# Block-sparse attention and a gated feed-forward on one core: probabilities turned by DMA transposes, a part of the value gathers issued by GpSimd

## The chip, the cores and the metric

One NeuronCore of a Trainium2 chip runs the whole program. The metric is the device time of one execution in microseconds (us). In the profile PE is TensorE, PEld its weight loads, DVE VectorE, ACT ScalarE, POOL GpSimd and SP SyncE. SP computes nothing here: it issues DMAs.

## The reference

```python
mask = np.abs(blk_i - blk_j) <= 1                       # blocks of 32 positions
mask = mask | (blk_i == 0) | (blk_j == 0) | (blk_i == 23) | (blk_j == 23)
for qb in range(24):
    for kb in sampled_blocks[qb]:                       # three random blocks each
        mask[qb * 32:(qb + 1) * 32, kb * 32:(kb + 1) * 32] = True
scores = np.where(mask, scale * (q @ k.T), -1e9)
attn = softmax(scores) @ v                              # 4 batches, 8 heads, 768 x 64
x = attn.transpose(0, 2, 1, 3).reshape(3072, 512)
out = (sigmoid(x @ w_gate) * (x @ w_val)) @ w_out       # 512 -> 1536 -> 512
```

A query block of 32 rows sees its neighbours, the first and the last block and three sampled blocks; the first and the last query block see everything.

## The kernel before, in words

**The attention of one batch.** Blocks 1 to 22 are done in eleven steps of two query blocks, named by their first block: a step of batch 1 that starts with block 4 is `1_4`. Per step, POOL copies the three sampled key blocks of each query block into a buffer KG beside the window and the two end blocks (`kw`, line 745; `kg`, line 729). PE makes the scores (`sc`, lines 790 and 801): 256 keys per query block, two PSUM banks of 128 rows (4 pairs of heads by 32 queries) each. DVE takes the row maxima (`mx`, 815), ACT the exponentials with their sums (`ex`, 826) into one of three buffers P, and DVE or ACT divides by the sums (`sl`, 850 and 848). The probabilities then have to stand with the keys on the partitions. In batches 0 to 2 PE does that with eight 128x128 transposes into PSUM (`tp`, 870), and DVE or ACT copies them to one of three buffers PTS (`te`, 876). In batch 3 one DMA transpose from P to PTS does it, issued by SP (line 858). Last PE multiplies with the values (`pv`, 888), and the result goes into XT or XL, the transposed input of the feed-forward (`xe`, 914).

**The values.** Each batch is written in token order to a DRAM tensor `scr` (615). V1A to V1D hold four windows of 96 rows each (`w`, 692), and V2A to V2D the sampled rows: for each query block three DMAs of 32 rows from `scr`, issued by SP, their addresses read from registers (`vg`, 762).

**The dense blocks.** Blocks 0 and 23 have scores against all 768 keys (`dsc`, 941), maxima, exponentials, a division (953, 959, 968), per block two sets of six PE transposes (`dtp`, 976; eight in batch 0) with a copy each to DPT (`dte`, 985), and a product with all values (`dpv`, 998; 1006 in batch 0). In batches 1 to 3 value tokens stand six to a partition, so that partition p holds tokens 6p to 6p+5 (eight in batch 0); the scores read the keys with that step and write them with the tokens of one slot together.

**Keys and queries** of batches 1 to 3 are loaded one or two batches ahead by POOL (437), put in row order (`rr`, 556, on POOL or DVE), turned on PE (571) and copied to KT and QT (586 to 590).

**The feed-forward** takes the tokens in nine groups of 1, 1, 2, 2, 2, 4, 4, 4 and 4 tiles of 128: twelve pairs of products with `wg` and `wv` (1061), a tanh (1070), a product on DVE (1075), then twelve products with `wo` per tile (1096), a scaling and the store (1110). A group can start only when all its tokens have been through the attention.

**The order** stands in a table, ORDER: one word per operation, its engine, and its buffers by number. Each engine executes its instructions in that order, and tile dependencies make it wait. A number after `+` is a count of filler matmuls ahead of an operation (line 1119), which compute nothing that is used.

Of the kernel before, what the change touches and what calls it, by code (L numbers as in the profile page):

```python
# [18 lines left out]
BLK = 32  # L19
# [44 lines left out]
sc0_12:P01 w0_8:G0 vg0_10:S rz0_8:D dxe0_0:A rz0_10:D sl0_100:D kg0_14:G sl0_101:A mx0_120:D0 vg0_9:S pv0_4:P1+5.7
sl0_80:D wg2:G tp0_10:P22 mx0_121:D xe0_4:A pv0_6:P0 sl0_81:D vg0_8:S ex0_120:A0 xe0_6:D vfl0D:G te0_10:D
pg0_2:P00+4.7 vg0_11:S pu0_2:P1 th0_2:A1 tp0_8:P10 kw0_16:D0 ex0_121:A pg0_0:P00 sc0_14:P03 th0_0:A0 h0_2:D w0_12:S0
kg0_16:G te0_8:A rz0_12:D pu0_0:P0 pg0_3:P10 h0_0:D mx0_140:D2 pu0_3:P0 sl0_120:A wv2:G kw0_18:D1 pv0_8:P1+1.7
kg0_18:G th0_3:A2 regSP0_1:S pg0_1:P10 h0_3:D xe0_8:A pv0_10:P2 mx0_141:D pu0_1:P0 ex0_140:A1 w0_16:G0 vg0_15:S wo0:G
th0_1:A1 xe0_10:A pg0_6:P10+4.7 h0_1:D sl0_121:D wo1:G ex0_141:A sc0_16:P21 vg0_19:S pu0_6:P0 kw0_1:G2 mx0_160:D6
pg1_3:P20 th0_6:A0 vfl0A:G th1_3:A2 pu1_3:P1 h0_6:D ex0_160:A2 pg1_5:P00 vg0_12:S h1_3:D rz0_14:D sc0_18:P30 th1_5:A1  # L70
pu1_5:P2 mx0_180:D4 sl0_141:A tp0_12:P10 pg1_6:P00 h1_5:D pu1_6:P1 te0_12:D regPOOL0_2:G th1_6:A0 pg1_10:P20 vg0_13:S
pu1_10:P0 th1_10:A2 mx0_161:D pg1_2:P20 h1_6:D th1_2:A1 wo2:G h1_10:D ex0_161:A pu1_2:P1+1.4 sl0_140:D vg0_14:S
pg1_0:P00 pu1_0:P2 h1_2:D kw0_2:D0 th1_0:A1 pg0_8:P10 ex0_180:A0 tp0_14:P21 h1_0:D kg0_2:G rz0_16:D sl0_160:D pu0_8:P0
vg0_17:S pg1_4:P20 sl0_161:D th0_8:A2 th1_4:A0 pu1_4:P1 mx0_181:D ldv10:G3 pg1_9:P20 tp0_16:P12 th1_9:A1 h0_8:D
te0_14:A pu1_9:P2 h1_4:D kw0_20:G1 pg0_7:P00 h1_9:D pu0_7:P1 te0_16:D kg0_1:G sc0_2:P13 th0_7:A1 pg0_4:P00 h0_7:D
mx0_20:D5 vg0_18:S pu0_4:P1 th0_4:A0 pg1_11:P20 vfl0B:G pv0_12:P1 mx0_21:D th1_11:A1 ex0_181:A pu1_11:P0 pg1_7:P20
h0_4:D vg0_16:S h1_11:D pu1_7:P1 xe0_12:D pg0_9:P00 th1_7:A0 sc0_1:P20 th0_9:A2 ex0_20:A1 ldk10:G2 rz0_18:D pu0_9:P0
h1_7:D pg1_1:P20 h0_9:D pu1_1:P1 kg0_20:G mx0_10:D1 pg1_8:P00 th1_1:A1 ex0_21:A pu1_8:P2 pv0_14:P1 h1_1:D sl0_180:D
pg0_10:P10 th1_8:A2 ldq10:G1 sl0_181:D th0_10:A0 tp0_18:P00 ex0_10:A2 h1_8:D w0_1:G0 mx0_11:D pu0_10:P1 sc0_20:P14
rz0_2:D sl0_20:D ex0_11:A py1_0:P2 regSP0_2:S mx0_200:D4 w0_2:G0 xe0_14:A h0_10:D te0_18:D ex0_200:A0 mx0_201:D  # L80
sl0_21:D ex0_201:A pv0_16:P2 rz0_1:D vg0_1:S sl0_10:D pg0_11:P10 xe0_16:D pv0_18:P0 th0_11:A0 pu0_11:P0 xe0_18:A
pg0_5:P10 sl0_11:D tp0_2:P11 vg0_3:S h0_11:D ys1_0:A0 vsh1:D0 dsc0_23:P20 th0_5:A1 pu0_5:P0 te0_2:A pg2_0:P20 vg0_20:S
h0_5:D dmx0_230:D6 pu2_0:P1 rrk1:G3 pg2_1:P00 th2_0:A2 pu2_1:P2 h2_0:D dex0_230:A1 dmx0_231:D3 pg2_4:P10 ldv20:G2
trk100:P1 th2_4:A2 trk102:P0 evk100:A regPOOL1_2:G pu2_4:P1 vg0_2:S tp0_1:P22 evk102:A h2_4:D trk101:P1 te0_1:D
pg2_2:P10 th2_1:A2 dex0_231:A0 trk103:P0 scr1:S h2_1:D py0_0:P0 vg0_21:S evk101:D evk103:A rrq1:G3 dsl0_231:D th2_2:A0
vg0_22:S kfl10:G kfl11:G rz0_20:D pu2_2:P2 sl0_200:D ys0_0:A1 trq102:P2 sl0_201:D trq101:P1 h2_2:D evq102:A trq100:P0
kw1_20:D0 pg2_5:P00 evq101:D kw1_1:G1 evq100:A trq103:P2 st0_0:S kg1_1:G pu2_5:P1 evq103:A dsl0_230:D tp0_20:P10
dtp0_230:P00 th2_5:A2 kg1_20:G te0_20:D gv1:S sc1_1:P41 dte0_230:A h2_5:D pg2_3:P20 mx1_10:D3 kw1_2:G1 st1_0:S
pu2_3:P1 th2_3:A2 mx1_11:D regSP1_2:S dtp0_231:P0 ldk20:G1 ex1_10:A1 pv0_2:P2 h2_3:D kg1_2:G dte0_231:D pv0_20:P1
xe0_2:A pg2_7:P20 xe0_20:D pv0_1:P0 regPOOL1_0:G th2_7:A1 pu2_7:P0 w1_1:G0 ex1_11:A vsh2:D3 pg2_9:P20 vg1_22:S  # L90
sc1_2:P02 xe0_1:A h2_7:D pu2_9:P1 kw1_4:G1 mx1_20:D5 pg2_6:P00 vg1_1:S kg1_4:G th2_9:A1 mx1_21:D sc1_20:P31 ex1_20:A2
pu2_6:P2 mx1_200:D2 kw1_6:G0 dpv0_23:P1 vfl1D:S th2_6:A0 h2_9:D kg1_6:G ex1_200:A0 mx1_201:D pg2_10:P00 scr2:S h2_6:D
ex1_21:A pu2_10:P1 rz1_1:D sl1_10:D pg2_8:P20 sl1_11:D th2_10:A2 sc1_4:P03 th2_8:A1 kw1_8:G1 pu2_8:P0 ex1_201:A
mx1_40:D7 w1_2:S0 rrk2:G2 tp1_1:P21 h2_10:D pg2_11:P20 ex1_40:A1 vg1_20:S rz1_20:D dxe0_23:D pu2_11:P1 h2_8:D
th2_11:A0 sc1_6:P10 ldq20:G1 rz1_2:D h2_11:D sl1_20:A pg3_1:P00 vg1_21:S mx1_41:D kg1_8:G pu3_1:P2 th3_1:A2 pg3_0:P10
sl1_21:D sl1_201:D tp1_2:P12 th3_0:A1 mx1_60:D6 pu3_0:P0 vg1_2:S te1_2:A py2_0:P1 kw1_10:D0 te1_1:D vfl1C:G ex1_60:A2
mx1_61:D ex1_41:A vg1_3:S h3_1:D h3_0:D ex1_61:A rz1_4:D kg1_10:G pg3_3:P20 sl1_41:D pv1_1:P0 sl1_200:D ys2_0:A1
sl1_40:D pu3_3:P0 regPOOL1_1:G th3_3:A2 rz1_6:D st2_0:S sl1_61:D sc1_8:P21 xe1_1:A gv2:S sc1_10:P05 kw1_12:G1
mx1_80:D4 pg3_4:P20 w2_2:G0 mx1_81:D tp1_20:P10 th3_4:A0 tp1_4:P01 ex1_80:A0 h3_3:D py2_1:P2 sl1_60:D kg1_12:G
regSP1_0:S mx1_100:D0 ex1_81:A mx1_101:D w1_4:G0 kw1_14:A0 te1_4:D vg1_6:S ex1_100:A1 kg1_14:G rz1_8:D te1_20:D  # L100
pv1_2:P2 ex1_101:A sl1_81:D pu3_4:P0 vg1_4:S w2_1:G0 sl1_80:D pv1_20:P0 xe1_2:A rz1_10:D pg3_2:P10 h3_4:D sl1_100:D
# [134 lines left out]
def kernel(  # L236
# [15 lines left out]
    def pin(x):  # L252
        return tc.keep_in_program_order(x)
# [251 lines left out]
    def pg_of(g):  # L505
        return bk(5, 6) if g < TUNE["two"] else pgb if g < len(GROUPS) - 2 else pgb + bk(4, 3, 2, 1, 0)
# [645 lines left out]
```

## Time and profile before

| | |
|---|---|
| median of 3 runs | 320.91 us (318.99 to 322.62) |
| the profiled execution, its own time | 320.9 us |
| its span, first to last instruction | 319.1 us |
| PE busy | 303.0 us (95% of the span) |
| DVE / ACT / POOL busy | 223.5 / 225.5 / 124.0 us |
| 16 DMA engines, share of the span: POOL's queue / SP's queue | 37.0% / 27.1% |

The span leaves 1.8 us of the execution's own time around it. A busy engine is one with an instruction in flight, and PE's matmuls overlap: a row of 0.61 us for eight transposes is the time from the first's start to the last's end, while the next matmul starts 0.45 us after the first. The chain of waits, which counts from start to start, is therefore the better price for work on PE. The DMA share of a stage is the time that its packets took, divided by 16 engines.

### The profile page before, as it was taken

Reading aid. Unit: us, or ns where it says so; the run is one execution under the profiler, and the core shown is the slowest. Engines: PE = TensorE matmul, PEld = TensorE weight load, DVE = VectorE, ACT = ScalarE, POOL = GpSimd, SP = SyncE. Lnnn points to the kernel's source line nnn. Section 1 sums busy time; section 2 is a strip of 40 time slices with the busy share of each in tenths; the row PEclk is TensorE's granted clock in tenths of the full one; section 3 lists DMA queues with packets and bytes.
Section 4 is the critical chain, followed back from the end, with each engine's and each line's share of the span. In section 5 each row is a group of like instructions: output and inputs, shape, how many; then the busy total and the mean of one; then the engine's idle time right before and its main releaser. Section 6 shows DMA issues by size and latency. Waiting matters only on the chain.

```text
span 319.1 us, 11300 instructions
## 1 busy us (share of the span) xinstructions
PE 303.0 (95%) x4015; PEld 186.3 (58%) x4015; DVE 223.5 (70%) x546; ACT 225.5 (71%) x666; POOL 124.0 (39%) x386
## 2 busy tenths in 40 slices
PE   7999649999999999999999999999999999999996
PEld 3545436867977777886555555556455544554443
DVE  4389435998999999886799788798876676113420
ACT  1469366898898989888799788799985765423411
POOL 7648955705877834815155222221322300000000
PEclk9999787999999999999999999999999999999999
DMA  7998999998699644999543302523455456811012
GB/s 113 206 240 160 230 228 222 215 230 191 135 273 189 202 129 124 160 208 192 165 154 98 106 16 65 178 72 77 116 143 133 98 126 145 159 68 68 0 49 83
DMA packets 50919, 45.99 MB, mean 144 GB/s; under 512 B 18096, under 2 KB 45616, under 8 KB 50768
## 3 DMA queue, kind: packets, MB, share of 16 engines
q0 software_dynamic: 18720, 21.43, 37.0%
q1 hardware_dynamic: 32144, 23.85, 27.1%
q8 instruction: 31, 0.51, 0.7%
q14 instruction: 24, 0.20, 0.2%
HBM read 47.10 MB, written 9.44 MB: 177 GB/s over the span
## 4 chain that ended last, share of the span: by engine, by line
PE 74%; DMA 10%; DVE 7%; ACT 6%; issue 2%; SPq 1%; POOL 0%; ACTq 0%; DVEq 0%; POOLq 0%
PE pall L1061 35%; PE pall L1096 18%; PE pall L888 5%; DMA V2D<-scr 4%; PE pall L801 3%; PE pall L870 3%; ACT P L826 3%; PE pall L571 2%; DMA V2C<-scr 2%; DMA stg<-in_k_dram 2%; DVE NM L815 2%; DMA scr<-XL 2%; PE pall L1119 2%; PE pall L941 2%; DVE P L850 1%
## 5 line engine op out<-in xcount | busy, mean ns | idle before, releaser
L826 ACT ACTIVATE P<-pall,NM 128x256 f16<-128x256 f32 x176 | 81.5, 481 | 5.3 <-DVE NM L815 3.2
L1075 DVE SCALAR_TENSOR_TENSOR HT<-TH,pall 128x512 f16<-128x512 f32 (+2 forms) x108 | 53.0, 504 | 34.4 <-PE pall L1061 24.7
L1070 ACT ACTIVATE TH<-pall 128x512 f32<-128x512 f32 (+2 forms) x108 | 48.5, 460 | 33.9 <-PE pall L1061 29.3
L729 POOL COPY KG<-KT 128x64 f32 x264 | 51.4, 244 | 49.1 <-PE pall L801 27.8
L1096 PE MATMUL pall<-wo,HT 128*128 128x512 f16 (+1 forms) x300 | 65.2, 371 | 0.6 <-DVE HT L1075 0.6
L815 DVE TENSOR_REDUCE NM<-pall 128x2 f32<-128x512 f32 x88 | 58.1, 682 | 5.6 <-PE pall L790 4.7
L1061 PE MATMUL pall<-XT,wv 128*128 128x256 f16 (+2 forms) x336 | 56.5, 291 | 0.9 <-DVE HT L1075 0.7
L1061 PE MATMUL pall<-XT,wg 128*128 128x256 f16 (+2 forms) x336 | 56.2, 291 | 0.4
L1061 PEld LDWEIGHTS <-wg 128*128 128x128 f16 x432 | 38.5, 99 | 26.4 <-issue 3.9
L1061 PEld LDWEIGHTS <-wv 128*128 128x128 f16 x432 | 37.5, 99 | 25.9 <-issue 5.0
L1096 PEld LDWEIGHTS <-HT 128*128 128x128 f16 x300 | 28.5, 98 | 31.3 <-DVE HT L1075 1.1
L826 ACT ACTIVATION_READ_ACCUMULATOR P<-pall,NM 128x1 f32 x176 | 37.3, 212 | 0.0
L850 DVE TENSOR_SCALAR P<-P,ZZ 128x256 f16<-128x256 f16 x140 | 34.8, 305 | 0.7
L1119 PE MATMUL pall<-WZ 128*128 128x512 f16 x83 | 23.2, 424 | 1.2 <-DVE WZ L390 1.2
L1061 PE MATMUL pall<-XL,wg 128*128 128x512 f16 x96 | 23.8, 379 | 0.0
L1061 PE MATMUL pall<-XL,wv 128*128 128x512 f16 x96 | 23.7, 379 | 0.0
L745 POOL COPY KG<-KT 128x384 f32<-128x384 f32 (+1 forms) x27 | 12.5, 475 | 23.5 <-PE pall L790 16.5
L914 ACT CAST XT<-pall 64x256 f16<-64x256 f32 (+1 forms) x48 | 16.3, 340 | 7.4 <-PE pall L888 6.8
L1105 ACT ACTIVATE YS<-pall 128x512 f32<-128x512 f32 (+1 forms) x18 | 10.4, 576 | 15.4 <-PE pall L1096 15.4
L870 PE MATMUL pall<-ident,P 128*128 128x128 f16 x264 | 20.1, 222 | 0.2 <-DVE DPT L985 0.2
L801 PE MATMUL pall<-KG,QT 64*32 64x256 f16 x704 | 18.2, 277 | 1.0 <-ACT DP L959 0.5
L959 ACT ACTIVATE DP<-pall,NM 128x768 f16<-128x768 f32 x16 | 14.4, 904 | 5.7 <-DVE NM L953 5.6
(102 smaller groups left out, 438.3 us busy)
## 6 DMA issues: line engine op xcount, KB each, us to landing
out_dram<-YS SPq DMA_DIRECT2D x23, 256.0 KB, 2.1
stg<-in_q_dram POOLq DMA_DIRECT2D x4, 768.0 KB, 9.4
stg<-in_v_dram POOLq DMA_DIRECT2D x4, 768.0 KB, 8.4
V2C<-scr SPq DMA_DIRECT2D x96, 32.0 KB, 3.0
V2D<-scr SPq DMA_DIRECT2D x78, 32.0 KB, 3.4
stg<-in_k_dram POOLq DMA_DIRECT2D x3, 768.0 KB, 9.2
scr<-stg SPq DMA_DIRECT2D x3, 768.0 KB, 3.4
V1C<-scr POOLq DMA_DIRECT2D x5, 384.0 KB, 4.1
```

The source lines that it names most:

```text
L729: pin(nc.gpsimd.tensor_copy(t[:, :, u, KO[r] + (2 + n) * BLK : KO[r] + (3 + n) * BLK].bitcast(f32), KT[r].bitcast(f32)[:, :, bass.ds(regs[ ...
L801: pin(nc.tensor.matmul(ts[hh][32 * p : 32 * p + 32, u * 256 + c0 : u * 256 + c1], QT[r][kp, p, i * BLK : (i + 1) * BLK], src, start=(merge ...
L815: pin(nc.vector.tensor_reduce(NM[pl.handles[hz][1]][:, 2 * hh : 2 * hh + 2], t, axis=AX.X, op=ALU.max, negate=True))
L826: pin(nc.scalar.activation(pb[:, hh, u, :], t[:, u * 256 : u * 256 + 256], AF.Exp, bias=NM[z][:, 2 * hh + u : 2 * hh + u + 1], scale=1.0, ...
L850: pin(nc.vector.tensor_scalar(pb[:, u, :], in0=pb[:, u, :], scalar1=z[:, 2 * hh + u : 2 * hh + u + 1], scalar2=None, op0=ALU.mult))
L870: pin(nc.tensor.transpose(t[:, m * 128 : m * 128 + 128], pb[:, hh, u, c * 128 : c * 128 + 128], ident))
L914: pin(copy(o)(dst[kp].rearrange("d a (u n) -> d u a n", n=BLK), s[kp, u0:u1]))
L1061: pin(nc.tensor.matmul(t, wt[:, c, f_ * 128 : f_ * 128 + 128], XT[g][:, c, :], start=(c == 0), stop=(c == 3)))
L1070: pin(nc.scalar.activation(TH[o.slots[ht][1]][:, 0:n], banks[pl.handles[hg][1]][:, 0:n], AF.Tanh, bias=0.0, scale=0.5))
L1075: pin(nc.vector.scalar_tensor_tensor(HT[:, f_, hoff : hoff + n], in0=TH[pl.handles[ht][1]][:, 0:n], scalar=1.0, in1=banks[pl.handles[hv][1 ...
L1096: pin(nc.tensor.matmul(t, HT[:, f_, hoff + tt * 128 : hoff + tt * 128 + 128], wo[:, f_, n0:n1], start=(f_ == 0), stop=(f_ == NF - 1)))
L1119: pin(nc.tensor.matmul(banks[o.spare], WZ[:, 0:128], WZ, start=True, stop=True))
```

## The change

Five things change, and the table of the order is new.

1. The probabilities of batches 1 and 2, too, are turned by one DMA transpose per step from SP (`turnby` 'PSSS'); PTS has four buffers in place of three.
2. The dense probabilities of batches 1 to 3 are turned by DMA transposes (`denseby` 'PSSS'): four per batch, 128x768 each, from DP straight into DPT. Batch 0 keeps PE.
3. For batches 1 to 3 the dense scores read 384 keys in a row and write them in a row; the exponential that follows reads PSUM with that step and writes the old order.
4. In batches 1 to 3 a gather of sampled values may be issued by POOL: one indirect DMA of 96 rows, with row numbers from a small table `gidx`, in place of three DMAs from SP. The new order does so for 36 of 66: 15, 12 and 9 in batches 1, 2 and 3.
5. Bank 7 joins the banks of the scores, and bank 4 those of the middle feed-forward groups.

By the new order, 15 of the windows of V1 are issued by SP (4 before) and 9 by POOL (20 before); of the six row-order copies, four are on DVE (all six were on POOL); 80 fillers stand in the table (83 before). `kqby` is 'PPPP', so that keys and queries go the old way.

```diff
- 'npt': 3,
- 'turnby': 'PPPS'}
+ 'npt': 4,
+ 'turnby': 'PSSS',
+ 'gather': 'SEEE',
+ 'denseby': 'PSSS',
+ 'kqby': 'PPPP'}

 ORDER = """
-wz:D cdma:S ldk00:G0 ldk01:G ldq00:G1 ldv00:G2 idx:D memset:G wg0:G mask:D wv0:G trk000:P1+12.7 trk001:P2 evk001:A
...
-    spool = bk(0, 1, 2, 3, 5, 6)
+    spool = bk(0, 1, 2, 3, 5, 6, 7)
...
-        return bk(5, 6) if g < TUNE["two"] else pgb if g < len(GROUPS) - 2 else pgb + bk(4, 3, 2, 1, 0)
+        return bk(5, 6) if g < TUNE["two"] else pgb + bk(4) if g < len(GROUPS) - 2 else pgb + bk(4, 3, 2, 1, 0)
...
+    def f_gix(o):
+        by = flat.rearrange("p (i n) -> p i n", n=3)
+        for n in range(3):
+            ps = slice(BLK * n, BLK * n + BLK)
+            pin(nc.vector.tensor_scalar(gtm[ps], in0=by[ps, :, n], scalar1=float(BLK), scalar2=float(-BLK * n), op0=ALU.mult, op1=ALU.add))
+            pin(nc.vector.tensor_tensor(gidx[ps], gtm[ps], pid[ps], op=ALU.add))
...
                 def f_vg(o, i=i, x=x, ws=ws, key=keys):
+                    if o.eng == "POOL":
+                        pin(nc.gpsimd.indirect_dma_start(V2[x][BLK:128, ws, :], None, scr[b][:, :],
+                                                         bass.IndirectOffsetOnAxis(ap=gidx[0 : 3 * BLK, i : i + 1], axis=0)))
+                        return
                     for n in range(3):
...
-                            ks = ks.rearrange("d (p j) -> d p j", j=TJ)[:, :, TJ // 2 * a : TJ // 2 * (a + 1)]
                             dst = t[32 * p : 32 * p + 32, a, 0:384]
-                            dst = dst.rearrange("q (j p) -> q p j", p=TP)
+                            if b:
+                                ks = ks[:, 384 * a : 384 * a + 384]
+                            else:
+                                ks = ks.rearrange("d (p j) -> d p j", j=TJ)[:, :, TJ // 2 * a : TJ // 2 * (a + 1)]
+                                dst = dst.rearrange("q (j p) -> q p j", p=TP)
...
+                    if b:
+                        dst = DP[o.slots[hDP][1]].rearrange("p (j a n) -> p a j n", j=TJ, a=2)
+                        src = src.rearrange("p a (n j) -> p a j n", j=TJ)
+                    pin(nc.scalar.activation(dst, src, AF.Exp, bias=NM[z][:, 0:1], scale=1.0, accum_out=ZZ[z][:, 0:1]))
...
+                if TUNE["denseby"][b] == "S":
+                    def f_dtd(o, hh=hh, e=e, hDP=hDP, hTS=hTS):
+                        dst = dturn(b, e, (o.slots if hTS in o.slots else pl.handles)[hTS][1])[:, hh]
+                        pin(nc.sync.dma_start(dst.rearrange("p (c n) -> p c n", c=TJ), DP[pl.handles[hDP][1]], transpose=True))
```

Three places of the new order, as the built programs have them (a tile's number after its name tells one buffer from another; ISA is a register instruction).

**SP, the first steps of batch 1, before.** Sampled rows go to V2D and V2C by line 762, the end blocks to V1D and V2D by 648, batch 2's values to `scr` by 615, windows by 692, and line 632 loads the end blocks for POOL's copies.

```order
L632 DMA GV<-scr_127 32x512 x2
L1110 DMA out_dram<-YS_124 128x512
L473 TENSOR_LOAD vidx x2
L762 ISA
L762 DMA V2D<-scr_127 32x512
```

**SP, the same steps, now.** L799 is the gather, L895 the transpose of a step, L724 a window, L680 the end blocks, L664 the ends for POOL's copies.

```order
L664 DMA GV<-scr_129 32x512 x2
L724 DMA V1C<-scr_129 96x2x512 x2
L895 DMA_TRANSPOSE PTS_119<-P_98 128x8x128
L724 DMA V1D<-scr_129 96x512 x2
L680 DMA V1C<-scr_129 32x4x512
L680 DMA V2C<-scr_129 32x4x512
L724 DMA V1A<-scr_130 96x2x512 x2
L895 DMA_TRANSPOSE PTS_117<-P_97 128x8x128
L895 DMA_TRANSPOSE PTS_116<-P_99 128x8x128
L724 DMA V1D<-scr_129 96x4x512
```

The eighteen gathers of these three steps (six query blocks) have left SP, and between the windows stand three transposes, each of which waits for its step's division; what is behind one on SP waits with it.

**SP, the end of batch 1's dense blocks, now.** L1018 is the new dense transpose; before, no instruction of SP belonged to the dense blocks.

```order
L1018 DMA_TRANSPOSE DPT_122<-DP_121 128x6x128
L1018 DMA_TRANSPOSE DPT_122<-DP_120 128x6x128
L895 DMA_TRANSPOSE PTS_116<-P_97 128x8x128
L488 TENSOR_LOAD vidx
L1163 DMA out_dram<-YS_127 128x512
L1018 DMA_TRANSPOSE DPT_122<-DP_121 128x6x128
L1018 DMA_TRANSPOSE DPT_122<-DP_120 128x6x128
```

The two DP buffers are used twice in a row: the second block's exponentials have to wait until the first block's transposes have read them.

**POOL, between the key copies of the fourth and fifth step of batch 1, now.** L761 is the copy of a sampled key block, L795 the indirect gather.

```order
L761 COPY KG_95<-KT_76 128x4x16
L795 DMA V2C<-scr_129,gidx 96x512
L795 DMA V2D<-scr_129,gidx 96x512 x2
L795 DMA V2C<-scr_129,gidx 96x512 x3
L761 ISA
L761 COPY KG_96<-KT_76 128x4x16
```

Six gathers have come in between two sets of key copies, so that the scores of the fifth step wait for them; before, one window copy of keys stood there.

281 lines of the change are left out of this document (152 added, 129 removed).

## The prediction

> **What bounds the kernel now.** I read the page first, then the busy time of each engine by stages of 25 us, then the chain of waits, then the groups of instructions by form, and last the issuing queues of SP and POOL. From the page:
>
> ```profile
> span 319.1 us, 11300 instructions
> PE 303.0 (95%) x4015; PEld 186.3 (58%) x4015; DVE 223.5 (70%) x546; ACT 225.5 (71%) x666; POOL 124.0 (39%) x386
> PE 74%; DMA 10%; DVE 7%; ACT 6%; issue 2%; SPq 1%; POOL 0%; ACTq 0%; DVEq 0%; POOLq 0%
> ```
>
> PE is busy for 95% of the span and holds 74% of the chain. An average can hide stages, so here they are (columns: stage, its length, busy us of PE, PEld, DVE, ACT, POOL with counts, granted clock, share of the DMA engines, GB/s):
>
> ```profile
> 60.00:85.00 25.00, 24.99 (x420) 19.37 (x405) 23.11 (x61) 21.28 (x63) 10.95 (x27) 1.00 0.98 203
> 85.00:110.00 25.00, 24.86 (x458) 18.55 (x457) 24.06 (x67) 23.59 (x86) 19.57 (x60) 1.00 0.93 209
> 110.00:135.00 25.00, 24.50 (x408) 18.84 (x406) 23.08 (x55) 22.63 (x61) 14.61 (x41) 1.00 0.62 135
> 135.00:160.00 25.00, 25.00 (x352) 16.95 (x350) 18.80 (x43) 20.87 (x56) 7.45 (x23) 1.00 0.82 190
> 160.00:185.00 25.00, 24.53 (x295) 13.69 (x293) 20.89 (x49) 21.69 (x65) 10.02 (x37) 1.00 0.40 114
> 260.00:285.00 25.00, 25.00 (x200) 12.79 (x198) 9.62 (x22) 12.68 (x38) 0.68 (x1) 1.00 0.55 126
> ```
>
> From 60 us on PE is never without a matmul for more than half a microsecond in 25, at the full clock. So PE's work sets the end, and what is taken from it comes off the time, as long as nothing else takes its place. Three things are near to doing so between 60 and 135 us, in batch 1: DVE (23 to 24 of 25), ACT (up to 23.6), and the DMA engines (0.98 and 0.93). After 160 us the DMA engines are half idle.
>
> **The turns of P leave PE.** The chain has a set of eight transposes as a piece of its own, and the dense ones, eight or twelve at a time:
>
> ```profile
> 53.38 0.45 PE pall L870 x8
> 84.99 0.45 PE pall L976 x8
> 154.34 0.78 PE pall L976 x12
> ```
>
> Batches 1 and 2 have 22 sets: 22 x 0.45 = 9.9 us off PE. The dense blocks of batches 1 to 3 have 72 transposes; by 0.45/8 they cost 4.0 us, by 0.78/12 4.7, and I take 4.3. The copies that go with them are off DVE and ACT:
>
> ```profile
> L876 DVE COPY PTS<-pall 128x1024 f16<-128x1024 f16 x24 | 16.4, 684 | 1.9 <-PE pall L870 1.7
> L876 ACT COPY PTS<-pall 128x1024 f16<-128x1024 f16 x9 | 9.2, 1017 | 0.7 <-PE pall L870 0.7
> L985 ACT COPY DPT<-pall 128x768 f16<-128x768 f16 x5 | 4.1, 811 | 0.7 <-PE pall L976 0.7
> L985 DVE COPY DPT<-pall 128x768 f16<-128x768 f16 x7 | 3.8, 550 | 0.0
> L603 DVE COPY stg<-stg 128x3072 f16<-128x3072 f16 x3 | 2.9, 955 | 0.0
> ```
>
> DVE loses 17 copies of 0.684 and 7 of 0.550 (15.5 us), and gets four row-order copies of the size of line 603's (3.8 us): 11.7 less. ACT loses 5 x 1.017 and 5 x 0.811: 9.2 less. I cost both at nothing, since PE covers them; what they give is room, so that DVE and ACT can follow a PE that is some 5% quicker through batch 1. Without them PE would be held at their 24 of 25 us there.
>
> **The dense scores read in order.** Rows of PE in time (start, length, matmuls), and the two forms by themselves (minimum, median and maximum in ns):
>
> ```profile
> 92.70 0.41 PE L801 MATMUL pall<-KG,QT 64*32 64x256 f16 x16
> 92.93 0.27 PE L790 MATMUL pall<-mrow,ones 64*32 64x192 bf16 x8
> ...
> 113.64 0.91 PE L941 MATMUL pall<-KT,QT 64*32 64x384 f16 x16
> 114.48 0.61 PE L1061 MATMUL pall<-XT,wv 128*128 128x256 f16 x4
> ```
>
> ```profile
> L941 PE MATMUL pall<-KT,QT x128: 479/493/520, 15.2 to 190.3; 64*32 64x384 f16 x128
> L801 PE MATMUL pall<-KG,QT x704: 266/269/418, 15.8 to 258.1; 64*32 64x256 f16 x176
> ```
>
> Sixteen matmuls over 384 stepped keys hold PE for 114.48 - 113.64 = 0.84 us; sixteen of 256 keys in a row, with the same operand rows, hold it for 0.23. At that rate 384 columns would take 0.35. No row shows 384 in order, and whether the step of the keys, that of the scores or neither makes it slow isn't seen, so six sets save between 0 and 6 x 0.49 = 2.9 us. I take 2.3, near the upper end, as the form in a row is the nearest row. The exponential's stepped read of PSUM has a near row as well: line 586, which gathers such a step out of PSUM on ACT, takes as long as line 985, which doesn't:
>
> ```profile
> L586 ACT COPY KT<-pall 128x768 f16<-128x768 f16 x11 | 8.6, 805 | 7.0 <-PE pall L574 6.7 <-PE pall L571 0.3
> ```
>
> That is 805 against 811 ns, so nothing. Three fillers fewer (0.6 us) lie ahead of 60 us, where PE waits for the DMA of weights and values anyway: nothing. The additional banks only loosen waits.
>
> **The transposes on SP and the DMA engines.** Batch 3 already has eleven:
>
> ```profile
> L858 SPq DMA_TRANSPOSE PTS<-P x11: 1231/1245/1997, 220.1 to 273.4; - x11
> DMA to landing us min/median/max: 2.7/2.8/5.0
> ...
> 240.60:241.70 1.10, 1.10 (x51) 0.62 (x49) 0.13 (x1) 0.54 (x1) 0.08 (x1) 1.00 1.06 238
> ```
>
> One holds SP's queue for 1.25 us, fills all 16 DMA engines for 1.10 x 1.06 = 1.17 us (the third row is a stage with one transpose in it), and has landed 2.8 us after its issue. On SP 22 more make 27.4 us, and 12 dense ones at three quarters of the size between 0.94 and 1.25 each, 11.2 to 15; eleven windows moved from POOL add some 0.4 each. What leaves is 36 gathers:
>
> ```profile
> L762 SPq DMA_DIRECT2D V2C<-scr x96: 315/316/1306, 24.6 to 276.6; - x96
> ...
> 218.72 1.31 SPq L762 DMA_DIRECT2D V2C<-scr  x3
> ```
>
> Three issues with their register work take 1.31 us (the second row, the three of one query block): 36 x 1.31 = 47 us. SP's queue is no fuller than it was. But a transpose waits at its head for the division, and behind it wait the windows and gathers of the next steps, which `pv` on PE needs; I count that into the waits below. The path of one step is longer: eight transposes and a copy (0.45 + 0.68) become 2.8 us or more. In batch 3 no PE wait is put down to a transpose, but there the DMA engines are at half load. How much traffic lengthens a landing is told by the gathers of 32 KB, in 60:85 and in 160:185 (share 0.98 and 0.40):
>
> ```profile
> DMA to landing us min/median/max: 2.1/4.9/6.3
> ```
>
> ```profile
> DMA to landing us min/median/max: 1.6/1.9/3.6
> ```
>
> Three microseconds more. So in batch 1 a transpose should take 3 to 6 us. What is late then is P itself: it has three buffers, and a step's exponentials wait on ACT until the transpose of three steps earlier has been read, with the feed-forward's tanh behind them, for which PE waits. A buffer is used 11/3 = 3.7 times in a batch; each use is 2.8 - 1.13 = 1.7 us longer in quiet, up to 4.9 in traffic. Over two batches that is between 0 (all of it in slack) and, in batch 1 with 4.9 and batch 2 with 1.7, 18 + 6 = 24 us. I take 4, near the lower end: P now waits for its place in PE's order too, and the four PTS buffers and the emptier DVE take up part of it.
>
> **The gathers on POOL.** Nothing in the trace is an indirect DMA. The near rows are POOL's plain DMAs (ns, minimum, median, maximum); the third row is the row-order copy:
>
> ```profile
> L692 POOL DMA_DIRECT2D V1C<-scr x9: 647/677/707, 24.9 to 265.1; - x9
> L692 POOL DMA_DIRECT2D V1D<-scr x9: 541/685/980, 31.0 to 254.5; - x9
> ...
> L556 POOL COPY stg<-stg 128x1536 f32<-128x1536 f32 x6 | 8.8, 1467 | 18.0 <-DVE stg L603 13.0 <-PE pall L571 2.9 <-PE pall L790 2.2
> ```
>
> From 0.54 us below to three plain ones above, 2.0 us; I take 0.9, a little over one plain DMA. Batch 1 is where it matters, with 15 of the 36. In 85:135 POOL is busy for 19.57 + 14.61 = 34.2 of 50 us. Four of its windows (2.7 us) and one row-order copy (1.5) leave; the stage gets some 7 us shorter with PE; so there are 13 us of room, and 15 x 0.9 = 13.5 just fill it. Cost: nothing at 0.9, and 15 x 1.1 = 16 us at 2.0.
>
> **The sum.** Against the span of the profiled execution: 319.1 - 9.9 - 4.3 - 2.3 = 302.6 us if PE stays without gaps, and 306.6 with 4 us of new waits. That execution took 1.8 us more than its span, 320.9, which is the median of the runs (320.91); so 304.4 without and **308.4 us** with the waits.
>
> **Rivals.** *A, all of PE's saving arrives*: 304.4 us. For it: PE has hardly a gap from 60 us on although DVE and ACT are nearly full, and both get emptier. Against it: the longer path above, in the stage with the most traffic.
>
> *C, the DMA engines become the bound in batch 1.* Their shares from 60 to 160 us make 24.5 + 23.3 + 15.5 + 20.5 = 83.8 of 100 us. Some 24 us of transposes (16.4 of batch 1, the rest of batch 2) fall into that time, which itself gets 8 us shorter: 108 in 92. Were all 16 us over to come before PE's operands, the time would be 304.4 + 16 = 320, so about 319 with a little slack, no change. For it: 0.98 and 0.93. Against it: much of the traffic there is loads of batches 2 and 3, which may slip past 160 us. The Trainium skill (DMA: Bandwidth & Descriptors, Queues, rings and completion order) says that each DMA engine takes turns between its queues, a packet at a time; by that a transpose beside a load takes about twice its time, and this case's gathers agree (4.9 against 1.9 us).
>
> *D, POOL becomes the bound in batch 1, slower than before.* If an indirect gather holds POOL for c us, batch 1 lacks 15c - 13 us, the key copies behind the gathers come late, the scores wait for them and PE with them. From c = 0.9 it costs, and from 2.2 it makes the time 304.4 + 20 = 324, slower by over 1%; at 2.5, 329 us. For it: 96 separate rows by index, and DVE nearly full beside it. Against it: POOL's plain DMAs of 96 to 384 rows took 0.54 to 0.98 us, those in the fullest stage too. The Trainium skill (SBUF — State Buffer, A bandwidth-pool intuition that's wrong) has a GpSimd DMA of 620 ns that takes 3100 under a DVE copy; by that the estimate would be 304.4 + 15 x 3.1 - 13 = 338 us. The trace doesn't agree for plain ones: the longest of line 692 on POOL is 0.98 us.
>
> **How the numbers follow.** The forecast (304.4 with 4 us of waits, 305 to 316) gets 0.48, A 0.27, C 0.14, D 0.11. A measurement of this kernel, whose runs lie within 0.6% of their median, can tell about 1% from no change: below 317.7 is faster, above 324.1 slower. The forecast and A are faster, and so is a part of C, 0.03: 0.78 faster, 0.11 the same, 0.11 slower. The range goes from 300 us (the dense scores' full 2.9 us, no waits, and some 3 us from the front of the program, whose order is new and isn't worked out here) to 320, C's upper end; that leaves out D and little else.
>
> **What would show it.** Right: 88 matmuls on the transposing line of P where there were 264, and 32 on the dense one where there were 104; 45 DMA transposes, in batch 1 landing in 3 to 6 us; sixteen dense scores in some 0.4 us; a PE without gaps from 60 us on, and a last feed-forward group that starts some 11 to 16 us earlier. Wrong by C: PE waits for transposes or for the load of batch 3's keys between 75 and 160 us, at a DMA share of 1. Wrong by D: gathers on POOL of 2 us or more, and PE waiting for key copies. The forecast fails if the sum of PE's gaps between 60 and 285 us grows by more than 12 us, or if the matmuls that remain get slower.

## The result, and the profile after

The changed kernel takes 338.11 us (335.07 to 339.15) where the kernel before took 321.56 in the same comparison (318.99 to 322.62): 1.0539 times as long, interval 1.0473 to 1.0605. Slower, where 308.4 was forecast. The profiled execution took 337.09 us. A median below is of all runs of a kernel, while a ratio leaves out runs that fell into a slower state, and is missing where too few are left.

From the page after; the first two rows are span and engines, the third SP's DMA queue (packets, MB, share of 16 engines), the last the shares of the chain:

```profile
span 335.3 us, 10562 instructions
PE 295.3 (88%) x3764; PEld 175.1 (52%) x3764; DVE 215.4 (64%) x526; ACT 217.7 (65%) x659; POOL 149.1 (44%) x409
...
q1 hardware_dynamic: 63584, 32.11, 43.7%
...
PE 56%; DMA 22%; ACT 9%; issue 6%; DVE 4%; SPq 1%; POOL 1%; another core or an unknown queue 0%; POOLq 0%; ACTq 0%; DVEq 0%
```

PE has less to do (295.3 us for 303.0) and stands still for longer: 335.3 - 295.3 = 40.0 us for 16.1. It holds 56% of the chain, no longer 74%; what it lost went to DMA, 22% for 10%. Against the sum's 302.6 us the span is 32.7 longer: 23.9 of idle time, and 8.8 of work (303.0 - 16.5 = 286.5 was the sum's).

The stages of 25 us say where (same columns as before):

```profile
60.00:85.00 25.00, 23.93 (x367) 18.37 (x363) 20.65 (x49) 21.16 (x62) 13.20 (x27) 1.00 1.19 219
85.00:110.00 25.00, 18.68 (x283) 13.83 (x281) 15.64 (x39) 14.45 (x51) 14.09 (x41) 0.86 1.08 202
110.00:135.00 25.00, 20.29 (x347) 13.98 (x345) 19.63 (x53) 18.96 (x63) 15.41 (x46) 1.00 0.93 169
135.00:160.00 25.00, 21.87 (x312) 16.17 (x311) 16.91 (x47) 16.27 (x50) 11.87 (x24) 0.86 1.08 201
160.00:185.00 25.00, 22.73 (x304) 12.85 (x302) 20.28 (x46) 21.00 (x60) 15.69 (x46) 1.00 0.89 190
```

PE idles in every stage, most in batch 1: 6.3 us from 85 to 110. DVE, ACT and POOL are all emptier than before in that stage, so none of them is the bound; the DMA engines are full or nearly so from 85 to 160 us (1.08, 0.93, 1.08 for 0.93, 0.62, 0.82). In two stages the clock is down. By finer stages, the first of these losses:

```profile
97.00:99.00 2.00, 0.00 (x0) 0.00 (x0) 1.27 (x3) 1.02 (x4) 1.70 (x2) 1.00 0.50 128
99.00:101.00 2.00, 0.98 (x8) 0.67 (x7) 1.54 (x4) 0.00 (x0) 1.39 (x3) 1.00 1.10 269
101.00:103.00 2.00, 0.99 (x24) 0.46 (x22) 0.88 (x4) 0.38 (x1) 1.88 (x7) 0.50 1.15 294
103.00:105.00 2.00, 1.84 (x11) 1.27 (x12) 1.49 (x5) 1.72 (x7) 1.61 (x7) 0.50 0.23 66
105.00:107.00 2.00, 2.00 (x14) 1.63 (x13) 2.00 (x8) 1.75 (x6) 0.60 (x1) 0.50 1.36 73
```

After 4 us in which PE was busy for 0.98, the clock is at half for 6 us: a gap is paid for twice. The Trainium skill (TensorE: Matmul & The Clock Gate, Part 1: The HAM clock gate) says that the array's clock is throttled to half by default and that activity releases it; the 0.50 agrees. It puts the idle window at about 3.4 us, and here no single gap was that long: the longest is the 2.84 us before 99.73. Two later falls of the clock, at 135.13 and 145.37 us, came after 3.4 us in which PE was busy for 1.51 and 1.13. So here little work was enough, not only none.

What that gap waited for, in the chain of waits (start, length):

```profile
82.31 14.03 DMA stg<-in_k_dram
...
96.36 0.96 DVE stg L571
97.33 0.60 DVE NM L852
...
98.66 0.70 DVE NM L852
...
99.73 0.60 PE pall L1114 x4
```

A load of the next batch's keys took 14.03 us; before, three such loads took 9.2 in the median (the last figure):

```profile
stg<-in_k_dram POOLq DMA_DIRECT2D x3, 768.0 KB, 9.2
```

Its row-order copy (line 571) now stands in DVE's queue ahead of the maxima of the scores (852), and a product on PE comes behind those. Three more pieces of the same chain are transposes:

```profile
169.51 5.62 DMA DPT<-DP
...
190.24 6.58 DMA PTS<-P
...
208.46 5.22 DMA PTS<-P
```

5 to 7 us where a transpose took 2.8 in batch 3 before. The waits between 60 and 290 us show little for P itself (engine, line and what it waited for; us, times, longest):

```profile
ACT DP L1003 <- DMA DPT<-DP: 5.9, 3, 2.5
...
ACT P L863 <- DMA PTS<-P: 1.2, 1, 1.2
...
PE pall L925 <- DMA PTS<-P: 2.5, 2, 1.8
...
DVE stg L571 <- DMA stg<-in_k_dram: 2.6, 1, 2.6
```

The two DP buffers of the dense blocks cost ACT 5.9 us, the P buffers only 1.2. PE waits 2.5 us for turned probabilities (line 925 is `pv`), and DVE 2.6 for the load of the keys.

The parts of the sum that can be read off one by one did what they should:

```profile
L907 PE MATMUL pall<-ident,P 128*128 128x128 f16 x88 | 7.6, 236 | 1.1 <-DVE P L887 0.5 <-DVE XT L951 0.3 <-ACT P L863 0.2
```

```profile
L981 PE MATMUL pall<-KT,QT x128: 319/333/520, 16.8 to 205.4; 64*32 64x384 f16 x128
```

```profile
L795 POOL DMA_INDIRECT V2C<-scr,gidx x14: 909/915/998, 94.2 to 283.7; - x14
```

88 transposes of P are left, a dense score of 384 keys in order takes 333 ns (493 stepped), and an indirect gather holds POOL for 0.92 us (0.9 taken).

### The profile page after: what moved, and what is told of

Same layout as the page of the kernel before. It is cut to its first block, busy times and chain, and to the rows that moved or that the text cites. A ratio compares the mean times of both kernels' runs of the same rounds, so it can differ in the third digit from the quotient of the medians.

```text
span 335.3 us, 10562 instructions
## 1 busy us (share of the span) xinstructions
PE 295.3 (88%) x3764; PEld 175.1 (52%) x3764; DVE 215.4 (64%) x526; ACT 217.7 (65%) x659; POOL 149.1 (44%) x409
## 3 DMA queue, kind: packets, MB, share of 16 engines
q1 hardware_dynamic: 63584, 32.11, 43.7%
## 4 chain that ended last, share of the span: by engine, by line
PE 56%; DMA 22%; ACT 9%; issue 6%; DVE 4%; SPq 1%; POOL 1%; another core or an unknown queue 0%; POOLq 0%; ACTq 0%; DVEq 0%
PE pall L1114 32%; PE pall L1149 12%; DMA PTS<-P 4%; ACT P L863 4%; DMA stg<-in_v_dram 4%; DMA stg<-in_k_dram 4%; PE pall L925 4%; PE pall L838 3%; DMA V1D<-scr 2%; PE pall L603 2%; DMA V2C<-scr 2%; DMA DPT<-DP 2%; DMA V2D<-scr 2%; ACT DP L1003 2%; DMA scr<-XL 1%
## 5 line engine op out<-in xcount | busy, mean ns | idle before, releaser
L1149 PE MATMUL pall<-wo,HT 128*128 128x512 f16 (+1 forms) x300 | 66.4, 377 | 0.0
L1114 PE MATMUL pall<-XT,wg 128*128 128x256 f16 (+2 forms) x336 | 58.1, 297 | 9.0 <-DVE NM L852 2.8
L761 POOL COPY KG<-KT 128x64 f32 x264 | 53.0, 250 | 17.7 <-issue 6.8
L1114 PE MATMUL pall<-XT,wv 128*128 128x256 f16 (+2 forms) x336 | 57.9, 297 | 1.5 <-DVE HT L1128 0.8
L1114 PEld LDWEIGHTS <-wv 128*128 128x128 f16 x432 | 39.1, 100 | 27.6 <-issue 3.9
L777 POOL COPY KG<-KT 128x384 f32<-128x384 f32 (+1 forms) x32 | 14.8, 475 | 44.4 <-PE pall L827 27.9
L838 PE MATMUL pall<-KG,QT 64*32 64x256 f16 x704 | 20.5, 282 | 6.9 <-ACT DP L1003 3.2
L1114 PE MATMUL pall<-XL,wg 128*128 128x512 f16 x96 | 23.9, 379 | 0.0
L1114 PE MATMUL pall<-XL,wv 128*128 128x512 f16 x96 | 23.8, 379 | 0.0
L1172 PE MATMUL pall<-WZ 128*128 128x512 f16 x80 | 22.6, 424 | 1.2 <-DVE WZ L394 1.2
L885 ACT ACTIVATE P<-P,ZZ 128x256 f16<-128x256 f16 x44 | 19.7, 509 | 2.5 <-DVE ZZ L872 2.5
L951 ACT CAST XT<-pall 64x256 f16<-64x256 f32 (+1 forms) x50 | 17.0, 339 | 6.8 <-PE pall L925 5.5
```

The lines of the kernel that those rows point to most:

```text
L761: pin(nc.gpsimd.tensor_copy(t[:, :, u, KO[r] + (2 + n) * BLK : KO[r] + (3 + n) * BLK].bitcast(f32), KT[r].bitcast(f32)[:, :, bass.ds(regs[ ...
L838: pin(nc.tensor.matmul(ts[hh][32 * p : 32 * p + 32, u * 256 + c0 : u * 256 + c1], QT[r][kp, p, i * BLK : (i + 1) * BLK], src, start=(merge ...
L885: pin(nc.scalar.activation(pb[:, u, :], pb[:, u, :], AF.Copy, scale=z[:, 2 * hh + u : 2 * hh + u + 1]))
L1114: pin(nc.tensor.matmul(t, wt[:, c, f_ * 128 : f_ * 128 + 128], XT[g][:, c, :], start=(c == 0), stop=(c == 3)))
L1149: pin(nc.tensor.matmul(t, HT[:, f_, hoff + tt * 128 : hoff + tt * 128 + 128], wo[:, f_, n0:n1], start=(f_ == 0), stop=(f_ == NF - 1)))
L1172: pin(nc.tensor.matmul(banks[o.spare], WZ[:, 0:128], WZ, start=True, stop=True))
```

## The experiments

Two theories stood at the start. By the one, transposes and gathers come late because the DMA engines and the queues are full, and buffers and in-order queues pass that on to PE. By the other, the operations themselves cost little, and the new table of the order is what makes PE wait. "Gaps" below is PE's idle time between 60 and 290 us in the profiled execution: 1.2 before, 23.8 after.

### One part alone, in the order of before

The dense scores alone (only the reads and writes of item 3):

```diff
+                            if b:
+                                ks = ks[:, 384 * a : 384 * a + 384]
```

> The kernel before, with the dense scores of batches 1 to 3 reading keys in order and nothing else changed. The prediction's term is -2.3 us (0 to -2.9): about 318.7 against 321, with the sixteen matmuls at 320 to 333 ns instead of 479 to 493. The rival is that DVE and ACT are what holds these stages, so that PE's saving is given back as gaps: no change, 320 to 322.

319.29 us for 320.66, ratio 0.9959 (0.9926 to 0.9992); gaps 1.5. PE's busy time:

```profile
PE 301.4 (95%) x4015; PEld 186.3 (59%) x4015; DVE 223.6 (70%) x546; ACT 225.2 (71%) x666; POOL 123.9 (39%) x386
```

1.6 us less work (303.0 before) and 1.4 us less time: where nothing else moves, PE's saving arrives. It is the one version with all of the work in it that comes out ahead of both kernels, by 0.4%, with an interval that ends just below 1.

P of batch 1 alone by transposes, with four PTS (operations stay in their places, the copies go):

```diff
- tp1_1:P21  - te1_1:D   ...
+ tp1_1:S2               ...
```

> The kernel before, with P of batch 1 alone turned by transfers (four PTS buffers), each transpose at the place in the order where PE's set stood. By the prediction's sum: 11 x 0.45 = 5 us less PE and most of the 4 us of waits, 319 to 321. Theory 'long path in traffic' (a transpose beside the loads takes 4 to 6 us, so P buffers come free late, ACT stalls on them and PE behind it): slower, 325 to 335, with PE gaps of 10 us or more between 75 and 135 us. Theory 'the new order and the row-order copies on DVE did it': 317 to 320, since neither is in this kernel.

357.69 us for 320.66, ratio 1.1092 (1.0994 to 1.119); gaps 32.3. ACT's wait, and the landing of transposes in batch 1:

```profile
ACT P L824 <- DMA PTS<-P: 25.3, 5, 8.3
```

```profile
DMA to landing us min/median/max: 2.8/5.2/11.3
```

The time is beyond the range of the theory that came nearest (325 to 335). The exponentials wait 25.3 us for a free P. The prediction's upper end for this batch was 18, from 4.9 us a use; but the landing has a tail of 11.3 us, and with three buffers the tail counts, not the median. By the Trainium skill (DMA: Bandwidth & Descriptors, Queues, rings and completion order) each DMA engine takes turns between its queues, a packet at a time; the estimate from that, about twice the time beside a load, agrees with the median (5.2 for 2.8), not with that tail.

P of batch 2 alone (`tp2_*` to SP in the same way):

> The kernel before, with P of batch 2 alone turned by transfers (four PTS buffers). By the sum 5 us less: 316 to 317. 'Long path in traffic' says the same within 2 us, since the DMA engines are half idle after 160 us: 316 to 318. If a transposed P costs more than it saves anywhere, whatever the traffic: 322 or more.

346.08 us for 320.66, ratio 1.0722 (1.0614 to 1.0831); gaps 20.8, in a stage in which the DMA engines are not full at all:

```profile
160.00:185.00 25.00, 18.80 (x198) 9.60 (x197) 11.73 (x32) 15.06 (x51) 8.78 (x32) 0.86 0.42 106
```

```profile
182.79 6.26 SPq L760 DMA_DIRECT2D V2A<-scr  x12
...
189.16 5.59 SPq L856 DMA_TRANSPOSE PTS<-P  x2
```

The second fence is SP's queue in time: two transposes stand behind twelve gathers, which for their part wait for a `pv` on PE. The transposes of the chain land in 2.7 to 2.8 us; they are issued late. So late landing is one part of the price, and the in-order queue of SP another.

The 36 gathers alone on POOL, in the places they had on SP:

```diff
- vg1_22:S
+ vg1_22:G
```

> The kernel before, with the 36 gathers on GpSimd at the same places of the order, and nothing else. The prediction's term is 0: 319 to 322. If it is the gathers that made the changed kernel slow (96 packets by index from GpSimd's queue beside the loads, or POOL late with the key copies), this one is slower by 4 us or more, with PE gaps between 75 and 160 us.

333.45 us for 320.66, ratio 1.0378 (1.029 to 1.0465); gaps 9.5, of which one of 6.5:

```profile
PE pall L818 <- POOL KG L742: 6.5, 1, 6.5
```

```profile
100.12 0.94 POOL L775 DMA_INDIRECT V2C<-scr,gidx  x1 [0.16 <-issue]
...
104.64 1.04 POOL L670 COPY V1C<-GV 32x1024 f32<-32x1024 f32 x1 [3.57 <-DMA out_dram<-YS]
```

A gather has left POOL after 0.94 us, as forecast. But then POOL waits 3.57 us before it can write the end blocks (line 670) into a window, and behind that copy stand the key copies (742) that PE's scores need. The view names a store of the output, which the copy doesn't need. By the semaphores that the copy waits on, in the trace's events, it waited for gathers that POOL itself had issued: two of them, issued at 97.88 and 100.12, had landed at 104.27 and 104.52, just ahead of the copy's start at 104.64. In the kernel before, the same copy waits on no DMA.

### What holds the queues

The fill moved ahead of the gathers into its buffer:

```diff
  mx1_40:D7
+ vfl1C:G
...
- vfl1C:G
```

> The kernel before with 36 gathers on GpSimd as in b_gather (333.5 us), but the fill of window C of batch 1 on GpSimd put ahead of the gathers into the same tile, three of which it waited for (3.6 us on GpSimd, 6.5 us of gap on PE, and a granted clock of 0.71 to 0.78 behind it). If that one wait is the cost: 319 to 323. If gathers by index cost by their traffic or by GpSimd's time: 329 to 334.

331.15 us for 320.81, ratio 1.0263 (1.0183 to 1.0344); gaps 7.9. It helped little, for the fill waits as before:

```profile
99.62 1.13 POOL L670 COPY V1C<-GV 32x1024 f32<-32x1024 f32 x1 [3.21 <-DMA V2D<-scr,gidx]
```

```profile
92.26 7.14 DMA V2D<-scr,gidx
```

It no longer stands behind the gathers into V2C, but it still waits for those into V2D, of which the last was issued at 92.26: 0.96 us of POOL, 7.14 us until it had landed. That the copy writes V1C and V2C, and none of it V2D, doesn't free it; why the build makes it wait wasn't tried. What costs in this wait is the landing, not the issue.

Seven P buffers in batch 1 instead of three (four of them in XL, which is free then):

```diff
+    PB += [XL[:, 2 * s : 2 * s + 2, :].rearrange("p a (c n) -> p a c n", c=2) for s in range(4)]
- ex1_200:A0
+ ex1_200:A3
```

> The kernel before with P of batch 1 turned by transfers as in b_p1 (357.7 us), and seven P buffers instead of three in batch 1. ACT waited 25 us there for P buffers that a transpose had not read yet. Theory 'buffers held': at least 20 of the 37 us come back, 322 to 337. Theory 'SP's queue and the landing' (PE waits for the turned P whatever the buffers): 345 to 358.

345.64 us for 320.81, ratio 1.0678 (1.058 to 1.0776); gaps 24.4. ACT's wait for P buffers is gone, and 12 of the 37 us with it. The rest has moved on to PE, in one piece:

```profile
151.94 1.24 SPq L857
...
153.63 9.28 DMA PTS<-P
...
162.95 1.06 PE pall L887 x16
```

One transpose took 9.28 us to land, and PE's product of that step waited 13.97 us in all. More buffers free ACT, but not the product.

Four DP buffers for the dense blocks of batch 1, in the changed kernel:

```diff
- dex1_230:A1   - dex1_231:A0
+ dex1_230:A2   + dex1_231:A3
```

> The changed kernel with four DP buffers instead of two in batch 1 (the two more lie in space that is free there), all transposes as they are. Theory 'buffers held': the wait of the dense exponentials for the transposes (two of 2.5 and 1.0 us in batch 1) goes and with it most of PE's gaps from 130 to 146 us: 329 to 333. Theory 'late landing' (dpv waits for the transposes anyway): 335 to 340.

327.75 us (323.21 to 329.37) for 320.81, some 10 less than the changed kernel, with no ratio; gaps 18.8. ACT's wait for DP falls from 5.9 to 2.4 us:

```profile
ACT DP L1003 <- DMA DPT<-DP: 2.4, 1, 2.4
```

### One part undone, in the order of after

Undone were: the row-order copies of batches 2 and 3's keys and 1 and 3's queries, back on POOL; the dense turns of batch 1, back on PE; both; P of batch 1, back on PE; and all 36 gathers, back on SP:

```diff
- rrk2:D0
+ rrk2:G0
...
- dtp1_00:S0
+ dtp1_00:P10 dte1_00:D
...
- tp1_1:S3
+ tp1_1:P03 te1_1:D
...
- vg1_21:G
+ vg1_21:S
```

> The changed kernel with all row-order copies of keys and queries on GpSimd again, at the same places of the order. Theory 'copies on DVE' (DVE waits in its queue for the late keys of batch 2, 82 to 97 us, and PE loses 5.6 us in gaps between 92 and 103 us and runs at a granted clock of 0.66 for the next ten): 326 to 332 against 338. Theory 'transposes and traffic' (the keys are late whoever copies them, and GpSimd then stands in DVE's place): 335 to 341.

> The changed kernel with the four dense transposes of batch 1 on PE again (32 matmuls, 1.8 us, and four copies). Theory 'dense path' (two DP buffers held by transposes and dpv two to five pieces of PE work behind them: PE's gaps between 120 and 146 us, 7 us): those gaps go, 331 to 334. Rival: the gaps there come from P's transposes on the same queue, so they stay: 337 to 341.

> The changed kernel with both: row-order copies on GpSimd and the dense transposes of batch 1 on PE. Alone they took 9 and 12 us off. If they are two separate stalls: 338 - 21 = 317, 314 to 320. If both only loosen one and the same stall (the traffic of batch 1): 323 to 327.

> The changed kernel with P of batch 1 turned on PE again (88 matmuls, 5 us, and eleven copies), batches 2 and 3 as they are. Theory 'P's transposes in traffic' (they hold P, crowd the loads and SP's queue): most of PE's 17 us of gaps between 85 and 165 us go, 325 to 331. If the copies on DVE, the gathers on GpSimd or the new order made the gaps: 338 to 345.

> The changed kernel with all gathers on SP again (36 more there, at 1.31 us each of SP's queue: 47 us). If gathers by index on GpSimd are what costs in this order too (12.8 us alone in the order of before): faster, 325 to 333. If SP's queue is the tight place beside the transposes: slower, 345 or more.

| undone | time, us | before | ratio (interval) | gaps, us |
|---|---|---|---|---|
| row-order copies | 328.64 (324.93 to 336.19) | 321.59 | none | 16.0 |
| dense turns of batch 1 | 326.08 (323.63 to 332.81) | 321.59 | 1.0179 (1.0053 to 1.0305) | 14.7 |
| both | 330.08 (327.52 to 331.88) | 320.81 | 1.0285 (1.0202 to 1.0369) | 16.7 |
| P of batch 1 | 331.66 (329.81 to 336.36) | 321.59 | 1.0336 (1.0204 to 1.0468) | 17.9 |
| gathers | 373.21 (371.81 to 377.59) | 321.59 | 1.1628 (1.1487 to 1.1769) | 43.6 |

Each of the first four gives 6 to 12 us back, and two together no more than one: their 330.08 lies above both ranges that were expected. (The dense turns of batch 1 are 24 matmuls on PE, not the 32 of the expectations.) So none of these numbers is "the share" of a part. They tell two things. First, no part of these alone makes the change slow: gaps of some 15 us or more stay whichever goes. Second, the parts hang together: with the transposes on SP, the gathers are better off SP. Alone on POOL they cost 12.8 us; back on SP they cost 35. In that kernel SP's queue holds 9% of the chain of waits, where it held 1%:

```profile
PE 44%; DMA 30%; SPq 9%; ACT 5%; DVE 5%; issue 5%; POOL 1%; POOLq 0%; ACTq 0%; DVEq 0%
```

That speaks against the second theory: four parts, one at a time in the old order, make -1.4, +37, +25 and +13 us, together far more than the 16.6 us of the whole change. By this comparison the new table hides most of what the operations cost. It doesn't clear the table, though: the order of before wasn't made for these operations, and the new order with all operations as before wasn't run.

### The traffic

Loads of batches 2 and 3 cut to one head of eight, in the changed kernel and, as a control, in the one before; and each transpose of P cut to 256 of 1024 columns. What is left out keeps old data, so these kernels show times and compute no usable output:

```diff
+                h1 = h0 + 1 if b > 1 else h1
```

```diff
-                    pin(nc.sync.dma_start(PTS[o.slots[hTS][1]],
-                                          PB[pl.handles[hP][1]].rearrange("p h u n -> p (h u n)"), transpose=True))
+                    pin(nc.sync.dma_start(PTS[o.slots[hTS][1]][:, 0:2],
+                                          PB[pl.handles[hP][1]].rearrange("p h u n -> p (h u n)")[:, 0:256], transpose=True))
```

> The changed kernel, with the loads of batches 2 and 3 cut to one of eight heads (the other heads keep old data; orders, waits and all other work are the same). Theory 'traffic': with some 28 us less of loads on the DMA engines between 60 and 185 us the keys of batch 2 and the transposes land early, PE's gaps from 85 to 175 us go and the clock with them: 310 to 320. Theory 'queues and order': 333 to 339.

> The control: the kernel before with the same cut of the loads of batches 2 and 3. PE has no gaps there, so both theories say no change: 318 to 322.

> The changed kernel, with each transpose of P (batches 1 to 3) reading and writing only the first 256 of 1024 columns (the rest of the turned P keeps old data; number, order and waits of the transposes are the same). Theory 'traffic': 33 transposes give back three quarters of their 1.2 to 2 us on all DMA engines and land earlier: 312 to 322. Theory 'queues and order': the waits ahead of the transposes on SP's queue stay, 330 to 338.

> The changed kernel with both cuts: the loads of batches 2 and 3 read one head of eight, and each transpose of P moves 256 of 1024 columns (the rest keeps old data). Theory 'traffic is all of it': the gaps nearly go and the time comes to the sum's 304.4 and the forecast's 308.4: 302 to 310. If waits in the in-order queues and the tight places of the new order remain without traffic: 313 to 322.

| kernel | time, us | before | ratio (interval) | gaps, us |
|---|---|---|---|---|
| changed, loads cut | 324.38 (320.87 to 329.57) | 320.41 | 1.0114 (1.0013 to 1.0216) | 18.6 |
| before, loads cut | 321.62 (320.35 to 323.94) | 320.41 | 1.0058 (1.0019 to 1.0097) | |
| changed, short transposes | 320.05 (316.73 to 323.19) | 320.41 | 0.9961 (0.9914 to 1.0008) | 13.9 |
| changed, both | 328.92 (328.22 to 335.01) | 321.48 | 1.0307 (1.0197 to 1.0418) | 18.7 |

The loads cost the kernel before nothing (it gets no quicker without them) and the changed one about 14 us. In the profile without them, of a run of 329.57 us, the row-order copy of the chain above starts with no wait, and the stage of the largest loss is whole:

```profile
91.17 0.95 DVE L571 COPY stg<-stg 128x3072 f16<-128x3072 f16 x1
```

```profile
85.00:110.00 25.00, 25.00 (x430) 18.68 (x421) 23.24 (x66) 22.12 (x81) 18.07 (x53) 1.00 0.86 204
```

The 18.6 us of gaps that are left lie in other stages; 7.0 of them are PE's waits for turned probabilities, for 2.5 in the changed kernel. Neither theory's range (310 to 320, 333 to 339) holds the time.

Shorter transposes take 18 us off, with SP's queue at 30.7% of the DMA engines for 43.7%:

```profile
q1 hardware_dynamic: 38240, 25.62, 30.7%
```

A short transpose still holds SP's queue for 1.20 us (1.27 before the cut; medians from 85 to 150 us), so what it gives back isn't time of the queue. Its own transfer is shorter as well, so this run alone doesn't tell its length from its competing with loads; the cut of the loads, with its control, does. So transposes and loads compete for the DMA engines, and taking away the loads, or most of each transpose, brings the time to within about 1% of before. But both together did not add up: the kernel with both came out slower than with either, and above both ranges that were expected. Its trace has stalls which most others lack, and for which no wait is recorded. In its chain of waits:

```profile
114.44 0.39 issue
114.82 0.22 PE pall L603
115.04 0.51 issue
115.55 0.27 PE pall L1114
115.82 0.46 issue
```

PE runs one matmul, then stands for some 0.4 us, for no reason that the profile shows. The changed kernel has the same at 120 us, where ACT and DVE stand still as well:

```profile
120.78 1.17 issue
121.95 0.38 PE pall L1114 x2
122.33 1.04 issue
123.37 0.38 PE pall L1114 x2
```

Between 60 and 290 us such stalls of PE come to 6.5 us in the changed kernel, 6.9 in this one, 1.4 with the gathers alone on POOL and at most 0.7 in the others. All but one of those two kernels' stalls (the changed kernel's at 66 us) lie among indirect gathers on POOL or within 3 us behind one, but kernels with the same gathers are free of them. What they are stays open.

### Other versions

Three parts undone at once, in the order of after: P and the dense turns of batch 1 on PE, and the row-order copies on POOL:

> The changed kernel with batch 1 as before: P and dense rows turned on PE (120 matmuls, 6.4 us more), row-order copies on GpSimd; batches 2 and 3 by transfers, gathers on GpSimd, the new order. Theory 'traffic in batch 1': 312 to 322 (the sum without gaps: 302.6 + 6.4 + 1.8 = 311). If the new order or the gathers on GpSimd cost by themselves: 324 to 332.

336.38 us for 320.41, ratio 1.053 (1.0423 to 1.0637); gaps 19.7. That is above both ranges, and more than with any of the three undone alone (326 to 332). So the traffic of batch 1's transposes can't be the whole cause. What else it is, this run doesn't show: the copies of the turns came back on DVE and ACT, and a fill on DVE, which takes 0.69 us in the changed kernel, took 2.21 here.

The dense scores in order, and only batch 3's dense blocks by transposes, where the DMA engines are half idle:

```diff
- dtp3_00:P10  - dte3_00:D  ...
+ dtp3_00:S0                ...
```

> The kernel before with the dense scores in order and the dense rows of batch 3 alone turned by transfers, between 185 and 235 us, where the DMA engines' share is 0.2 to 0.4: 24 transposes of PE less (24 x 0.78 / 12 = 1.6 us) on top of b_score's -1.4. If transfers pay where there is room: 316 to 319, ratio 0.985 to 0.994. If DP buffers or dpv wait for them there too: 320 to 325.

321.07 us for 321.48, ratio 1.0039 (0.9995 to 1.0083); gaps 3.6. PE has 299.6 us of work, 1.8 less than with the scores alone, and the gain doesn't arrive: even here a landing ends a wait of PE.

```profile
PE pall L1014 <- DMA DPT<-DP: 1.0, 1, 1.0
```

## Why the prediction was wrong, point by point

**PE's savings: right.** With each matmul counted from its start to the next one's, the lines of P's turns lost 9.5 us (9.9 was forecast), those of the dense turns 4.5 (4.3) and the dense scores 1.6 (2.3): 1.0 us short in all. The counts came as forecast, 88 and 32 matmuls left and 45 DMA transposes.

**The new waits: the step that failed.** "I take 4, near the lower end": PE's idle time grew by 23.9 us, 22.6 of them between 60 and 290 us. That P waits for its place in PE's order too, that there are four PTS buffers and that the DVE is emptier was to take up part of the longer path; it didn't in the one run that had the transposes of batch 1 alone, in the old order, with four PTS buffers, which cost 37 us. And the price counted buffers of P only. That 23.9 lies at the upper end of its own range, 24, is luck: that end was the price of P's buffers. In the changed kernel the P buffers are a small wait (1.2 us); the landing came through in three other places: two DP buffers (5.9 us on ACT), PTS itself before `pv` (2.5 us on PE), and the row-order copy on DVE behind a 14.03 us load (2.6 on DVE, 2.84 on PE). That copy was costed at nothing because DVE had room. It had; what it lacked was its operand. The prediction's own sign of failure, gaps that grow by more than 12 us, came.

**The matmuls that remain: put at nothing.** PE's busy time fell by 7.7 us where the three terms took 15.5 off, so the rest got 7.8 us slower; this too the prediction had named as a sign of failure, without a term for it. In the two stages with a clock of 0.86, PE's 18.68 and 21.87 us would have been 16.1 and 18.8 at full clock, so by this estimate 5.7 of the 7.8 are clock, lost behind gaps. A sum that adds waits to an unchanged busy time is too low once gaps come in a row.

**The gathers on POOL: duration right, term wrong.** 0.92 us for the 0.9 taken, and the longest of all 36 took 1.70, though DVE was busy for more than half of every stage from 85 to 285 us. The Trainium skill's 3100 ns for a GpSimd DMA beside a DVE copy (SBUF — State Buffer, A bandwidth-pool intuition that's wrong) isn't seen here, and rival D fell by its own price. But "nothing at 0.9" was wrong in the old order: alone they cost 12.8 us there, of which the one wait that was followed, 6.5 us on PE, came from their landing, on which POOL's fill waits in order.

**Rival C: the nearest, and not the whole.** DMA shares of about 1 from 60 to 160 us, PE waiting behind a load of keys (batch 2's, not batch 3's) and behind transposes, as it said. Its 16 us would have made 319; it had no price for the queues and the clock, and its gathers in traffic took 2.6 times their quiet time (4.9 for 1.9), not twice. That the traffic is a cause is shown by the cut of the loads (-13.7 us, and nothing in the kernel before); the short transposes (-18.1) point the same way. That it is the only one is not: with both cuts 328.9 is left, with stalls of unknown cause.

**Still open.** What the stalls without a wait are; what the new order costs by itself; and, with them, how the 32.7 us divide between landing, queue order and stalls. Undoing one part of the changed kernel (the gathers apart) or giving it two more DP buffers gives 6 to 12 us back whichever it is, so a sharper division can't be had from these runs.

## What to carry to other kernels

A DMA that replaces work of a busy engine is priced by its landing under the traffic of its own stage, tail included (here 2.8 us in quiet, up to 11.3 in a full stage), and for every in-order queue that comes to wait on it, not only for the buffers that it holds. A queue can make it dear where the DMA engines aren't full: batch 2's transposes cost 25 us, with a DMA share of 0.42 in their first stage. In a stage where the engines and the DMA are both near full, ask that before summing what is saved, and add the clock that PE can lose behind gaps.

## What the runs showed of the hardware

- An indirect gather of 96 rows of 1 KB, issued by GpSimd, holds the engine for 0.91 to 1.0 us as a rule (1.70 at most), 0.68 being the median of a plain one there; one of 7.14 us to landing stood in a chain of waits.
- A DMA transpose of 128x1024 took 2.8 us to land in quiet and up to 11.3 beside loads. It holds SP's queue for about as long with 256 columns as with 1024 (1.20 and 1.27 us, medians).
- A matmul with 384 moving columns takes 333 ns read and written in order, 493 ns read and written with a step (medians); which of the two steps costs wasn't told apart.
- PE's clock went to half for 6 us after 4 us of which it was busy for 0.98, with no gap above 2.84 us; two other falls came after 3.4 us with 1.51 and 1.13 busy.
